# Polysketch attention into a squared-ReLU MLP: an earlier load and turn of q's second part, and two token tiles of kv sums ahead of the first q features

## The chip, the core and the metric

The kernel runs on one core of one Trainium2 chip. Five engines work beside each other, each on its own instruction stream in order: TensorE (PE, matrix products), VectorE (DVE), ScalarE (ACT), GpSimd (POOL) and SyncE (SP), which here issues nearly all DMA transfers. They wait for each other on semaphores. The metric is device time in microseconds; what is told of a kernel is the median of several runs.

## What is computed

```python
def phi(x):
    a = np.einsum('rd,bhsd->bhsr', S1, x)
    b = np.einsum('rd,bhsd->bhsr', S2, x)
    return np.einsum('bhsi,bhsj->bhsij', a, b).reshape(*x.shape[:-1], r * r)
q_p, k_p = (phi(q), phi(k))
kv = np.einsum('bhsf,bhsd->bhfd', k_p, v)
z = np.sum(k_p, axis=2)
num = np.einsum('bhsf,bhfd->bhsd', q_p, kv)
den = np.einsum('bhsf,bhf->bhs', q_p, z)[..., None] + 1e-06
attn = num / den
x = attn.transpose(0, 2, 1, 3).reshape(B * S, H * D)      # 4352 x 128
h = np.maximum(x @ w_in, 0.0)                              # w_in 128 x 2048
out = (h * h) @ w_out                                      # w_out 2048 x 128
```

There are 4 batches, 4 heads, 1088 tokens and a head size of 32; the sketches have r = 8 rows, so a token has 64 features. All inputs and the output are 32-bit floats.

## The kernel before, in words

The MLP runs over ten chunks of tokens (256, 384, 448, 448, five of 512, 256). A chunk's 2048 hidden columns are cut into units. For each unit TensorE makes x @ w_in into a PSUM tile (`pg`, line 589), ScalarE takes the ReLU (`gt`, line 598), ScalarE or VectorE squares it (`g`, lines 609 and 611), and TensorE adds its product with w_out to the chunk's sum (`po`, line 630). The attention of one batch is made beside the MLP of the tokens before it, and its result is the transposed input `xT`.

**The start, written out by hand** (lines 682 to 823). Nothing of the MLP can run before the first 256 tokens of batch 0 have gone through attention, and that needs the sums over all 1088 tokens of k and v. So the start is one chain over small pieces:

- SP issues the loads in this order: S2, k of batch 0 in two parts, the first 256 columns of q, v in eight parts (four for token tiles 0 to 3, four for tiles 4 to 8), then two quarters of w_in, a quarter of w_out, q's second part (columns 256 to 640, line 184), the rest of w_in and w_out, q's last part. Later loads follow as the planner places them. Eight semaphores are used in turn for the transfers: a transfer is issued once the one eight places before it has landed.
- `keep_warm(n)` puts n dummy products on TensorE: W0 of them first, W1 after the sketch matrices are made (line 692), W3 before the first MLP product.
- VectorE turns k (`a_kT0`, line 284, three pieces) and q's first part (`a_qT(0, 0, 8)`, line 290).
- TensorE makes the k features of the nine token tiles in four groups of 2, 2, 3 and 2 (`a_kf`, line 309); ScalarE copies one half of each (`kb`, line 315), VectorE multiplies the halves (`a_kp0`, line 325).
- `q0` (line 743) makes the sketches of the first 256 q tokens into the PSUM tile `x0`, ScalarE copies a part (`qb0`, line 754), VectorE multiplies (`qp0`, line 761).
- `a_kv0(t)` (line 389) adds one token tile's features times v to the PSUM tile `kvp`, four products for each tile.
- From `kvp`, VectorE makes `bd` (line 775) and `zm` (line 785), TensorE the denominators and numerators (`den0`, `num0`, line 798), VectorE turns, inverts and spreads the denominators (`dT0`, `rd0`, `bc0`, lines 816 to 820) and multiplies: `xT` for tokens 0 to 255 (line 821).
- POOL casts the four quarters of w_in (`cast_wi`, line 674).

The PSUM tiles of the start share two tags, `po` and `pg`, with two buffers each: a new tile of a tag waits for the readers of the tile two before it.

**The rest is planned.** A small list scheduler (`_Order`) gets tasks with an engine, an estimated duration, a key and dependencies, simulates the engines by these estimates, and emits the instructions in the order of that simulation; on the chip each engine then keeps that order. A batch's queries are handled in chunks (`AC`): batch 0 in blocks of 8, 12 and 16 (a block is 32 positions). For the chunk (0, 8): `qT` turns (line 290), sketches `qc` on TensorE (line 297), turns `qt` (475), denominators `pd`, `dn`, `rc` (481 to 495), sixteen small copies `rd` on POOL (line 503), shuffles (512) and products (527) for `qp`, numerators `nd` on TensorE (542), two turns `bc` of the inverted denominators (552), and two products into `xT` (559). These last feed the second MLP chunk, whose first `pg` product of width 384 needs both.

The task `qT` of the third chunk (0, 20) turns q's last part in two pieces (256 and 192 columns). In the order of before they stand between the two `bc` turns of chunk (0, 8).

Of the kernel before, what the change touches and what calls it, by code (L numbers as in the profile page):

```python
# [9 lines left out]
F32 = mybir.dt.float32  # L10
# [4 lines left out]
def _ap(t: bass.AP, p0: int, np_: int, off: int, free):  # L15
    p = list(t.ap)[0]
    return bass.AP(
        t.tensor, t.offset + p0 * p[0] + off, [[p[0], np_]] + [list(d) for d in free]
    )
# [85 lines left out]
def kernel(  # L105
# [11 lines left out]
    nc = tc.nc  # L117
# [7 lines left out]
    GT, G2, LA = 4, 6, 3.5  # L125
    LU = 4
    KC = [(0, 160), (160, 128)]
    W0, W1, W3 = 5, 4, 1
    ND, QT, WI, KL, QL = 2, 3.0, (1.0, 1.9), (30.0, 8.0), 4.0


# [4 lines left out]
    FC, at = [], 0  # L136
# [16 lines left out]
    psf = ctx.enter_context(tc.tile_pool(name="psf", bufs=2, space=bass.MemoryType.PSUM))  # L153
# [3 lines left out]
    def sb(name, cols, dt=F32, rows=128):  # L157
        return cpool.tile([rows, cols], dt, tag=name, name=name)
# [10 lines left out]
    s_nat, ss, s2f = sb("s_nat", 32, rows=16), sb("ss", 80), sb("s2f", 32)  # L169
# [13 lines left out]
    def load_q(eng, b, c0, c1):  # L183
        eng.dma_start(
            qn[b % 2][:, c0:c1],
            bass.AP(q.tensor, q.offset + b * H * S * D + c0, [[G * D, 128], [1, c1 - c0]]),
        )
# [16 lines left out]
    def load_wi(eng, c):  # L204
        eng.dma_start(
            w_in32[:, 512 * c : 512 * c + 512], moe_w_in[:, 512 * c : 512 * c + 512]
        )

    def load_wo(eng, c):
        eng.dma_start(  # L210
            _ap(w_o, 0, 128, 512 * c, [[128, 4], [1, 128]]),
            bass.AP(
                moe_w_out.tensor, moe_w_out.offset + c * 512 * 128,
                [[128, 128], [128 * 128, 4], [1, 128]],
            ),
        )
# [51 lines left out]
    st = {}  # L268

    def att(name):  # L270
        return psa.tile([128, 2048], F32, tag="att", name=name)

    def banks(t_, x, col, n, k=2):

        return _ap(t_, 0, 128, 512 * x + col, [[512, k], [1, n]])
# [5 lines left out]
    def a_kT0(t0, n):  # L281
        p = 3 if t0 + n > NT - 2 else 4
        i = 32 * (first(0, t0, 1) - first(0, t0, 0))
        nc.vector.transpose(
            _ap(kt0, 0, 128, 128 * t0, [[32, p], [128, n], [1, 32]]),
            _ap(kn[0], 0, 128, 32 * first(0, t0, 0), [[i, p], [32, n], [1, 32]]),
        )

    def a_qT(b, i0, n):
        nc.vector.transpose(qT[:, 32 * i0 : 32 * i0 + 32 * n], qn[b % 2][:, 32 * i0 : 32 * i0 + 32 * n])  # L290
# [31 lines left out]
    def a_kp0(t0, n):  # L322

        kf, kb = st["kf", t0]
        nc.vector.tensor_tensor(
            out=_ap(st[0, "kp"], 0, 128, 256 * t0, [[64, 4 * n], [8, 8], [1, 8]]),
            in0=_ap(kf, 0, 128, 0, [[8, 4 * n], [1, 8], [0, 8]]),
            in1=_ap(kb, 0, 128, 0, [[8, 4 * n], [0, 8], [1, 8]]),
            op=mult,
        )  # L330
# [55 lines left out]
    def a_kv0(t):  # L386
        for h in range(H):
            i, y, o, o_v = h % 2, h // 2, 64 * (H * t + h), 32 * (NT * h + t)
            nc.tensor.matmul(  # L389
                st[0, "kvp"][64 * i : 64 * i + 64, 64 * y : 64 * y + 64],  # L390
                st[0, "kp"][:, o : o + 64],
                _ap(vn[0], 0, 128, o_v, [[VC - o_v, 2], [1, 32]]),
                start=(t == 0 and y == 0),
                stop=(t == NT - 1),
                skip_group_check=True,
            )
# [171 lines left out]
    for ci, (c0, n) in enumerate(FC):  # L568
        first_unit[c0] = len(units)
        nb = 512 // n  # L570
# [120 lines left out]
    for h in range(H):  # L691
        nc.tensor.matmul(
            sp[32 * h : 32 * h + 32, 0:80], s_nat[:, :], sel[:, 80 * h : 80 * h + 80]
        )
    nc.scalar.copy(ss[:, :], sp[:, 0:80])
    load_wi(nc.sync, 0)
    load_wi(nc.sync, 1)
    load_wo(nc.sync, 0)
    load_q(nc.sync, 0, 256, 640)
    load_wi(nc.sync, 2)  # L700
    load_wi(nc.sync, 3)
    for c in range(1, 4):
# [29 lines left out]

    a_kT0(4, 3)
    a_kT0(7, 2)
    a_qT(0, 0, 8)


    x0 = att("x0")

    def q0(x):  # L740
        for y in range(2):
            r, o = slice(64 * y, 64 * y + 64), 512 * (2 * x + y)
            nc.tensor.matmul(x0[:, o : o + 256], sq[r, 128 * x : 128 * x + 128], qT[r, 0:256])  # L743

    new_kp(0)
    qb0 = wpool.tile([128, 512], F32, tag="qb0", bufs=1, name="qb0")
# [2 lines left out]
    a_kf(2, 2, psf, "pg")  # L749
    a_kf(4, 3, psf, "po")  # L750
    a_kf(7, 2, psf, "pg")
    q0(0)
    q0(1)
    nc.scalar.copy(_ap(qb0, 0, 128, 0, [[256, 2], [1, 256]]), banks(x0, 0, 0, 256))
    st[0, "kvp"] = psf.tile([128, 512], F32, tag="pg", name="kvp")
    for t0, n in ((0, 2), (2, 2), (4, 3), (7, 2)):
        a_kp0(t0, n)
        for t in range(t0, t0 + n):
            a_kv0(t)

    nc.vector.tensor_tensor(
        out=_ap(qp0, 0, 128, 0, [[256, 2], [1, 256]]), in0=banks(x0, 2, 0, 256),
        in1=_ap(qb0, 0, 128, 0, [[256, 2], [1, 256]]), op=mult,
    )
    nc.vector.transpose(s2f[:, :], _ap(ss, 0, 128, 72, [[0, 4], [1, 8]]))
    den0 = psf.tile([128, 512], F32, tag="po", name="den0")
    for y in range(2):
        nc.tensor.matmul(
# [5 lines left out]
    def a_bd(x):  # L774
        nc.vector.tensor_tensor(
            out=_ap(bd, 0, 128, 128 * x, [[64, 2], [32, 2], [1, 32]]),
            in0=_ap(st[0, "kvp"], 0, 128, 32 * x, [[64, 2], [0, 2], [1, 32]]),
            in1=_ap(own_p, 0, 128, 0, [[0, 2], [1, 2], [0, 32]]),
            op=mult,
        )  # L780
# [8 lines left out]
        op=mult,  # L789
    )  # L790
    a_bd(0)
    st["kvt"] = wpool.tile([128, 128], F32, tag="kvt", name="kvt")
    nc.scalar.copy(st["kvt"][:, :], st[0, "kvp"][:, 0:128])
    num0 = psf.tile([128, 512], F32, tag="pg", name="num0")
# [49 lines left out]
    def on(f, *args):  # L844
        return lambda eng: f(*args)

    prev = {"qc": None}
    PEL, M, T0 = 0.3, 5.0, 1.5
# [5 lines left out]
    def q_tasks(b, i0, nb, key):  # L854

        m = 16 * nb
        k0 = key - 6.0 - 8 * dve(m)
        names = []
        for x in range(2):
            i1, n1 = i0 + x * (nb // 2), nb // 2  # L860
            n1 = min(n1, G - i1)
            names.append(("qT", b, i1))
            O.add(
                names[-1], {"DVE": dve(32 * n1)}, k0 - 1.5,
                ([("qn", b)] if b else []) + prev["qTuse"], on(a_qT, b, i1, n1),
                at=QT if i0 == 20 else 0.0,
            )
        kb = KB.get((b, i0))
        O.add(
            ("qc", b, i0), {"PE": 0.75}, k0 - 1.0,  # L870
            names + [("w", b)] + ([("kT", kb, 0), ("kT", kb, 18)] if kb else []),
            on(a_qc, b, i0, nb), rings=[("att", 1)], lag=PEL,
        )
        if kb:
            glued(("kc", kb), 0.65, ("qc", b, i0), lambda eng: a_kc(kb, st[b, "qc", i0]))
        prev["qTuse"] = [("qc", b, i0)] if i0 + nb == 4 * NT else []
        for x in range(2):
            O.add(
                ("qt", b, i0, x), {"DVE": dve(m)}, k0 - 0.3 + 0.1 * x, [], on(a_qt, b, i0, nb, x),
                uses=[("qc", b, i0)], rings=[("qt", 1)] if x == 0 else [],  # L880
            )
        rc = [("rc", b, j) for j, _ in AC[b] if j < i0] or [("rc", b - 1, j) for j, _ in AC[b - 1]]
        O.add(
            ("pd", b, i0), {"DVE": dve(8 * nb)}, k0 - 0.1, rc, on(a_pd, nb),
            uses=[("qt", b, i0, 0), ("qt", b, i0, 1)],
        )
        O.add(
            ("rc", b, i0), {"DVE": 0.2 + nb * 17 / 960}, k0 - 0.1, [], on(a_rc, nb),
            uses=[("pd", b, i0)], rings=[("rc", 1)],
        )  # L890
        for c in range(4):
            O.add(
                ("rl", b, i0, c), {"POOL": 0.8}, k0 + 0.1 * c, [], on(a_rl, b, i0, nb, c),
                uses=[("rc", b, i0)], rings=[("rd", 2)] if c == 0 else [],
            )
        for w_ in ("qb", "qa0", "qa1"):
            for x in range(2):
                O.add(
                    (w_, b, i0, x), {"DVE": dve(m)}, k0, [], on(a_qs, b, i0, nb, w_, x),
                    uses=[("qc", b, i0)], rings=[(w_, 1)] if x == 0 else [],  # L900
                )
                k0 += 0.1
        for e in range(E):
            for x in range(2):
                O.add(
                    ("qp", b, i0, e, x), {"DVE": dve(m)}, k0 + 2.0, [], on(a_qp, b, i0, nb, e, x),
                    uses=[(f"qa{e}", b, i0, x), ("qb", b, i0, x)],
                    rings=[("qp", 3), ("qp", 3)] if (e, x) == (0, 0) else [],
                )
                k0 += 0.1  # L910
# [124 lines left out]
    for u in range(NU):  # L1035
# [9 lines left out]
        for i in range(m):  # L1045
# [3 lines left out]
                rings=[("pg" if u else "po", 2)] if i == 0 else [], lag=0.05,  # L1049
# [3 lines left out]
            rings=[("gt", GT)],  # L1053
# [13 lines left out]
        for j, mm in enumerate(mm2s):  # L1067
# [3 lines left out]
                rings=[("po", 2)] if d0 + j == 0 else [], lag=0.05,  # L1071
# [3 lines left out]
        if d0 + m == NB and ci != last:  # L1075
            po = [x for u_ in range(first_unit[c0], u + 1) for x in pe2[u_]]
            O.add(("oT", c0), {"DVE": dve(n)}, tu[u] + 3.0, [], on(f_oT, c0, n), uses=po,
                  rings=[("oT", 2)])
# [47 lines left out]
```

## Time and profile before

| what | value |
|---|---|
| median of 3 runs | 186.29 us (185.88 to 187.98) |
| time of the profiled execution | 185.68 us |
| its span, first to last instruction | 183.9 us |
| outside the span | 1.8 us |
| busy: PE, PE weight loads | 178.4 us (97%), 105.4 us (57%) |
| busy: ACT, DVE, POOL | 137.8 us (75%), 121.2 us (66%), 39.0 us (21%) |
| granted TensorE clock over the span | 1.000 |
| HBM read, written | 8.78 MB, 2.23 MB |

The profile is one execution, taken by the hardware profiler. Its page gives busy times and shares of the engines, the span in 40 equal slices of 4.6 us with the busy share in tenths, the chain of work that ended last, and the costliest groups of instructions. From the trace one can ask for a timeline (start, duration, engine, line, operation, tiles; instructions that follow each other are merged with a count, and the idle time before them with what ended it stands in brackets), for the waits by engine, and for single lines. Since a TensorE product overlaps the next, its start says more than its duration.

### The profile page before, as it was taken

The page shows a single profiled execution, that of the slowest core. Times are in us where ns is not written, and L with a number is a line of the kernel's source. Part 1 is how long each engine was busy: PE and PEld are TensorE (multiplying, and loading weights), DVE is VectorE, ACT ScalarE, POOL GpSimd, SP SyncE. Part 2 cuts the span into 40 slices and gives each one's busy share as a digit, 9 for nine tenths or more (in the row PEclk, how much of TensorE's full clock was granted, in tenths as well). Part 3 has the DMA queues.
Part 4 walks back from the last instruction along what each step waited for, and adds up shares of the span by engine and source line. Part 5 has one row for each costly group of instructions (what it writes and reads, how often), then busy time and mean ns, then how long its engine had stood idle before and what let it go on. Part 6 is the DMA issues. An engine that isn't in the chain of part 4 may idle for free.

```text
span 183.9 us, 3989 instructions
## 1 busy us (share of the span) xinstructions
PE 178.4 (97%) x1526; PEld 105.4 (57%) x1526; DVE 121.2 (66%) x258; ACT 137.8 (75%) x261; POOL 39.0 (21%) x157
## 2 busy tenths in 40 slices
PE   8989999989999999999999999999999999999992
PEld 2748766656555566555464554545555545555792
DVE  4969859989999972699996334997343334333640
ACT  3339969948958887699937778894777777777990
POOL 4526308418500001660008100510000000000000
PEclk9999999999999999999999999999999999999999
DMA  5799991020039700000030300003003000300121
GB/s 153 186 311 337 270 252 54 0 32 4 0 52 234 172 2 4 0 5 0 0 54 0 57 0 5 0 0 49 10 4 57 0 0 5 52 0 0 30 31 29
DMA packets 24610, 11.26 MB, mean 61 GB/s; under 512 B 17936, under 2 KB 23056, under 8 KB 24592
## 3 DMA queue, kind: packets, MB, share of 16 engines
q1 hardware_dynamic: 24416, 10.95, 25.4%
q8 instruction: 12, 0.20, 0.5%
q10 hardware_dynamic: 176, 0.07, 0.1%
q14 instruction: 6, 0.05, 0.1%
HBM read 8.78 MB, written 2.23 MB: 60 GB/s over the span
## 4 chain that ended last, share of the span: by engine, by line
PE 94%; DVE 1%; POOL 1%; ACT 0%; issue 0%
PE po L630 59%; PE pg L589 18%; PE nd L542 4%; PE po L625 2%; PE pol L625 2%; PE qc L297 2%; PE nd L407 1%; PE warm L681 1%; PE kvp L389 1%; PE qc L341 1%; PE kvp L407 1%; PE x L743 1%; POOL irep L715 1%; POOL sq L708 0%; DVE xT L559 0%
## 5 line engine op out<-in xcount | busy, mean ns | idle before, releaser
L630 PE MATMUL po<-g,w_o 128*128 128x512 f32 (+3 forms) x288 | 122.4, 546 | 0.0
L598 ACT ACTIVATE gt<-pg 128x512 f32<-128x512 f32 (+3 forms) x145 | 75.7, 568 | 31.1 <-PE pg L589 30.7
L630 PEld LDWEIGHTS po<-g,w_o 128*128 128x128 f32 x288 | 53.5, 189 | 31.0 <-issue 24.2
L589 PE MATMUL pg<-xT,w_in 128*128 128x512 f32 (+3 forms) x160 | 70.6, 521 | 0.4 <-DVE xT L821 0.4
L609 ACT ACTIVATE g<-gt 128x512 f32<-128x512 f32 (+2 forms) x104 | 61.8, 621 | 1.7
L611 DVE TENSOR_TENSOR g<-gt 128x512 f32<-128x512 f32 (+2 forms) x41 | 29.3, 716 | 38.9 <-ACT gt L598 38.1
L589 PEld LDWEIGHTS pg<-xT,w_in 128*128 128x128 f32 x160 | 29.2, 190 | 29.4 <-ACT gt L598 12.1
L503 POOL COPY rd<-rc 32x9 f32<-32x9 f32 (+2 forms) x80 | 19.2, 240 | 27.8 <-DVE rc L495 24.6
L449 POOL COPY kv<-kvt 32x64 f32<-32x64 f32 x48 | 12.5, 261 | 45.3 <-DVE kvt L426 43.1
L512 DVE STREAM_SHUFFLE qa<-qc 128x576 f32<-128x576 f32 (+2 forms) x20 | 11.8, 647 | 0.0
L527 DVE TENSOR_TENSOR qp<-qa,qb 128x576 f32<-128x576 f32 (+2 forms) x20 | 10.8, 600 | 0.0
L475 DVE STREAM_TRANSPOSE qt<-qc 128x576 f32<-128x576 f32 (+2 forms) x10 | 5.8, 609 | 6.9 <-PE qc L341 5.2
L360 DVE TENSOR_TENSOR kp<-fs 128x576 f32<-128x576 f32 x12 | 8.6, 740 | 0.0
L634 DVE STREAM_TRANSPOSE oT<-po 128x512 f32<-128x512 f32 (+3 forms) x9 | 5.9, 653 | 2.3 <-PE po L630 2.3
L542 PE MATMUL nd<-qp,kv 32*32 32x288 f32 (+2 forms) x320 | 6.8, 353 | 0.0
L559 DVE TENSOR_TENSOR xT<-nd,bc 128x576 fp32r<-128x576 f32 (+2 forms) x10 | 5.6, 602 | 1.8 <-PE nd L407 1.0
L290 DVE STREAM_TRANSPOSE qT<-qn 128x192 f32<-128x192 f32 (+3 forms) x11 | 6.0, 561 | 1.0 <-DMA qn<-in_q_dram 1.0
L512 DVE STREAM_SHUFFLE qb<-qc 128x576 f32<-128x576 f32 (+2 forms) x10 | 6.1, 649 | 0.0
L542 PEld LDWEIGHTS nd<-qp,kv 32*32 32x32 f32 x320 | 3.8, 103 | 3.7 <-issue 2.2
L552 DVE STREAM_TRANSPOSE bc<-rd 128x576 f32<-128x576 f32 (+2 forms) x10 | 5.7, 595 | 0.3 <-POOL rd L503 0.3
L625 PE MATMUL po<-w_o,g 128*128 128x128 f32 x32 | 5.8, 279 | 0.0
L625 PE MATMUL pol<-w_o,g 128*128 128x128 f32 x32 | 5.7, 275 | 0.0
(101 smaller groups left out, 89.2 us busy)
## 6 DMA issues: line engine op xcount, KB each, us to landing
kn<-in_k_dram SPq DMA_DIRECT2D x3, 544.0 KB, 7.1
qn<-in_q_dram SPq DMA_DIRECT2D x3, 544.0 KB, 9.1
vn<-in_v_dram SPq DMA_DIRECT2D x9, 144.0 KB, 7.8
w_in<-in_moe_w_in_dram SPq DMA_DIRECT2D x4, 256.0 KB, 5.3
w_o<-in_moe_w_out_dram SPq DMA_DIRECT2D x4, 256.0 KB, 5.4
out_dram<-oT SPq DMA_DIRECT2D x12, 64.0 KB, 2.0
out_dram<-oT SPq DMA_DIRECT2D x8, 56.0 KB, 2.7
out_dram<-oT SPq DMA_DIRECT2D x8, 48.0 KB, 1.9
```

What stands on the lines that cost most here:

```text
L360: nc.vector.tensor_tensor(out=_ap(st[b, "kp"], 0, 128, 64 * NT * h, [[64, NT], [8, 8], [1, 8]]), in0=_ap(fs, 0, 128, o, [[32, NT], [1, 8], ...
L449: nc.gpsimd.tensor_copy(_ap(st[b, "kv"], 32 * c, 32, 64 * h, [[32, E], [1, 32]]), _ap(st["kvt"], 32 * h, 32, 0, [[64, E], [1, 32]]),)
L503: nc.gpsimd.tensor_copy(st[b, "rd", i0][32 * h : 32 * h + 32, n * c : n * c + n], st["rc"][32 * c : 32 * c + 32, n * h : n * h + n],)
L512: nc.vector.stream_shuffle(in_=banks(st[b, "qc", i0], 2 * x, 0, m), out=_ap(st[b, which, i0], 0, 128, 2 * m * x, [[m, 2], [1, m]]), mask=m ...
L527: nc.vector.tensor_tensor(out=st[b, "qp", i0, e][:, r], in0=st[b, f"qa{e}", i0][:, r], in1=st[b, "qb", i0][:, r], op=mult,)
L542: nc.tensor.matmul(nd[32 * h : 32 * h + 32, 512 * c : 512 * c + m], kv[r, o : o + 32], qp[r, m * h : m * h + m], start=(e == 0), stop=(e = ...
L589: nc.tensor.matmul(st["pg", u][:, n * i : n * i + n], w_in[:, 128 * (d0 + i) : 128 * (d0 + i) + 128], xT[:, c0 : c0 + n],)
L598: nc.scalar.activation(gt[:, 0:w], st["pg", u][:, 0:w], Relu)
L609: nc.scalar.activation(to, of, Square)
L611: nc.vector.tensor_tensor(out=to, in0=of, in1=of, op=mult)
L625: nc.tensor.matmul(po[x // 128][:, 0:128], g[:, x : x + 128], w, start=(d == 0), stop=(d == NB - 1),)
L630: nc.tensor.matmul(po[0][:, 0:n], w, g, start=(d == 0), stop=(d == NB - 1))
```

## The change

Five things are edited. (1) The load of q's second part is issued ahead of the first two quarters of w_in and the first quarter of w_out, not behind them. (2) It is turned in one piece (384 columns) by hand, behind `a_bd(0)` in the start, and the planner's two `qT` tasks of chunk (0, 8) are left out; its `qc` task gets an earliest time of 0.4 in the planner. (3) The kv sums of the first two token tiles go ahead of `q0`, with the turn of q's first part between their feature product and the next; `kvp` takes a buffer of the tag `po`, not `pg`. (4) The turn of S2 (`s2f`) moves from behind `qp0` to the place where q's first turn was. (5) One dummy less ahead of the k features (W1), one more ahead of the first MLP product (W3).

```diff
-    W0, W1, W3 = 5, 4, 1
+    W0, W1, W3 = 5, 3, 2
...
+    load_q(nc.sync, 0, 256, 640)
     load_wi(nc.sync, 0)
     load_wi(nc.sync, 1)
     load_wo(nc.sync, 0)
-    load_q(nc.sync, 0, 256, 640)
     load_wi(nc.sync, 2)
...
     a_kT0(7, 2)
-    a_qT(0, 0, 8)
+    nc.vector.transpose(s2f[:, :], _ap(ss, 0, 128, 72, [[0, 4], [1, 8]]))
...
-    q0(0)
-    q0(1)
-    nc.scalar.copy(_ap(qb0, 0, 128, 0, [[256, 2], [1, 256]]), banks(x0, 0, 0, 256))
-    st[0, "kvp"] = psf.tile([128, 512], F32, tag="pg", name="kvp")
+    st[0, "kvp"] = psf.tile([128, 512], F32, tag="po", name="kvp")
     for t0, n in ((0, 2), (2, 2), (4, 3), (7, 2)):
         a_kp0(t0, n)
+        if t0 == 0:
+            a_qT(0, 0, 8)
         for t in range(t0, t0 + n):
             a_kv0(t)
+        if t0 == 0:
+            q0(0)
+            q0(1)
+            nc.scalar.copy(_ap(qb0, 0, 128, 0, [[256, 2], [1, 256]]), banks(x0, 0, 0, 256))
...
-    nc.vector.transpose(s2f[:, :], _ap(ss, 0, 128, 72, [[0, 4], [1, 8]]))
...
     a_bd(0)
+    a_qT(0, 8, 12)
...
-        for x in range(2):
+        for x in range(0 if (b, i0) == (0, 8) else 2):
...
-            on(a_qc, b, i0, nb), rings=[("att", 1)], lag=PEL,
+            on(a_qc, b, i0, nb), rings=[("att", 1)], lag=PEL, at=0.4,
```

What becomes of the planned part, read from the two built programs: TensorE's and POOL's orders stay the same but for the edits above. VectorE and ScalarE differ in one stretch. Before, VectorE has `bc`, `qT` (256), `qT` (192), `bc`, `xT`, `xT`; after, it has `bc`, one square `g` of 128x512, `bc`, `qT` (256), `qT` (192), `xT`, `xT`. That square, of the seventh unit of the first chunk, was ScalarE's before.

## The prediction

> **What bounds the kernel now.** I read the page first: engine rows by slice, then the chain that ended last.
>
> ```profile
> span 183.9 us, 3989 instructions
> PE   8989999989999999999999999999999999999992
> PE 94%; DVE 1%; POOL 1%; ACT 0%; issue 0%
> ```
>
> TensorE is busy in nearly every slice, and the change leaves its work alike but for one dummy moved. So only idle TensorE time can be won or added. The waits of TensorE (total, times, longest) show how little there is:
>
> ```profile
> PE warm L681 <- PEq L1110: 0.8, 1, 0.8
> PE qc L297 <- DVE kvt L426: 0.5, 1, 0.5
> PE pg L589 <- DVE xT L821: 0.4, 1, 0.4
> PE qc L297 <- ACT gt L598: 0.4, 1, 0.4
> PE x L743 <- POOL sw L721: 0.2, 1, 0.2
> ```
>
> The first lies at the start-up barrier and the second at 40 us, outside the edits: about 1.0 us is in reach. The last two releasers are misnamed: `qc` and `x` need a turn of q, as the timeline (start, duration) shows.
>
> ```profile
> 5.77 0.45 DVE L290 STREAM_TRANSPOSE qT<-qn 128x256 f32<-128x256 f32 x1 [0.30 <-DMA qn<-in_q_dram]
> 6.14 2.71 DVE L325 TENSOR_TENSOR kp<-kf,kb 128x512 f32<-128x512 f32 x4
> 6.36 1.14 PE L743 MATMUL x<-qT,sq 64*128 64x256 f32 x8 [0.24 <-POOL sw L721]
> ...
> 13.37 0.64 DVE L290 STREAM_TRANSPOSE qT<-qn 128x192 f32<-128x192 f32 x2 [0.70 <-DMA qn<-in_q_dram]
> 13.89 0.61 PE L297 MATMUL qc<-qT,sw 32*32 32x96 f32 x32 [0.37 <-ACT gt L598]
> 13.93 1.13 DVE L611 TENSOR_TENSOR g<-gt 128x256 f32<-128x256 f32 x2
> 14.02 1.52 POOL L674 CAST w_in<-w_in 128x512 fp32r<-128x512 f32 x2 [1.17 <-DMA w_in<-in_moe_w_in_dram]
> ...
> 19.20 0.37 DVE L552 STREAM_TRANSPOSE bc<-rd 128x192 f32<-128x192 f32 x1
> 19.50 0.66 DVE L290 STREAM_TRANSPOSE qT<-qn 128x256 f32<-128x256 f32 x2
> 20.48 0.38 DVE L552 STREAM_TRANSPOSE bc<-rd 128x192 f32<-128x192 f32 x1 [0.33 <-POOL rd L503]
> 20.79 0.58 DVE L559 TENSOR_TENSOR xT<-nd,bc 128x192 fp32r<-128x192 f32 x2
> 21.52 0.41 PE L589 MATMUL pg<-xT,w_in 128*128 128x384 f32 x1
> ```
>
> `x` starts 0.14 behind the first turn's end (6.22), `qc` behind the first half of the second (about 13.75); that turn waits for its load. Last, `xT` ends at 21.37 and the second chunk's first product starts 0.15 later: VectorE already gates TensorE there.
>
> **The start, to xT.** The first kv sums now stand ahead of `x` on TensorE and need all four first v loads. Its sequencer reached that wait early in the trace:
>
> ```profile
> L389 PEldq EVENT_SEMAPHORE  x2: 51/84/117, 6.4 to 6.5; - x2
> ```
>
> The wait at 6.50 took 117 ns where the other took 51, so it ended at 6.62, when the fourth load was in. These loads are issued as before. The feature product is earlier: it can start at 5.6 (behind the k turns that end at 5.47 and the turn of S2, 0.19) and takes 0.65. So v ends the wait, and TensorE starts at about 6.69, not 6.36: 0.33 lost. `x` and every later kv sum are queued behind it. Part returns: before, kv sums started at 7.44, after `x` had issued (eight passes of 0.108, to 7.23), because their buffer waited for the second feature product; that 0.2 is gone. The sum: 6.69, 16 of the 72 passes at 0.0295 (2.1 us over 71) to 7.16, `x` to 8.03, 0.05 for the switch, 55 passes to a last start at 9.70, against 9.54. The start is late by 0.16; with v in at 6.2, the feature product sets 6.36 less 0.02 and it is early by 0.18. I take +0.16, as the load order ahead of v is unchanged.
>
> What hides the rest: the k features start on the k turn (first piece done 4.63, they start 4.78), so the dummy removed there gains nothing; the added one (0.22 in a run of them) ends at about 12.65, ahead of `xT` at 12.83. The moved `s2f` has its slot before 5.6. `qp0` is done near 9.65, ahead of `kvp`. The hand-made turn (about 0.5, between 0.45 for 256 columns and 0.65 for 512) starts near 10.5, and `dT0` waits for denominators until about 11.1. Its cover is its load: in the first place of w_in, which took 4.1 us from issue at 6.36, 192 KB against 256, it lands between 9.8 and 10.5. If later than 10.6, every microsecond is paid.
>
> On SP the load passes three others, which move one slot (0.47) back and wait for other semaphores. By their old landings read against bytes (256 KB at 10.5, 512 at 12.2, 768 at 12.8, 960 at 13.35) the w_in quarters land at about 11.8 and 12.7. The cast of 0.61 ends at 12.4, needed at 12.9; the second at 13.35, needed at 14.1; w_out by 13.35, needed at 14.5. No cost, but margins of 0.5, not 2. POOL's order is unchanged.
>
> **qc.** Its 0.37 wait goes. `qc` starts at about 13.62, 0.27 earlier, with `xT` 0.16 later. That does not last: ScalarE's ReLUs are back to back from the first product on, so all are 0.16 late, and the product of the sixth unit, which needs the fourth unit's ReLU (end 15.58, then 15.74), issues at about 15.89, as before. Net zero.
>
> **VectorE behind it.** Two turns (0.64) leave ahead of the squares. The second square took 830 ns, the first 382; it started at 14.23, inside the cast from 14.02, and ended 0.27 behind that cast's end at 14.79, which is 256 columns' worth. With the start 0.16 late it could go at 14.10, again behind the cast's start, and ends as before. So everything down to `rc` and POOL's copies stands where it stood.
>
> **The new order of VectorE.** The second `bc` waits for POOL's copies, to 20.45. Before, both turns of q's last part filled that wait. Now a 512 square fills it, and the turns stand behind `bc` and ahead of `xT`: by spacing of starts, 0.33 and 0.295, together **0.62**. Queued behind are `xT` and the product of width 384, and all of TensorE behind that. ScalarE's freed 0.6 buys nothing there.
>
> **The square's price on POOL.** The trace has no 512 square beside these copies. Nearest rows: POOL's copies of the same line, alone, and beside products with two SBUF inputs:
>
> ```profile
> L503 POOL COPY rd<-rc x16: 182/186/192, 45.2 to 48.6; 32x9 f32<-32x9 f32 x16
> L503 POOL COPY rd<-rc x16: 178/296/1097, 27.4 to 33.4; 32x4 f32<-32x4 f32 x16
> ```
>
> The 1097 started beside the 1.21 us sum at L382. The square would start at 19.5 with four copies still to come. Bounds: 0, if POOL keeps its pace, and 0.53 (512 columns at the rate of the 0.27 above). I take 0.4, by the 1097. Nothing earlier than 20.45 follows from either; below zero is excluded, as the square gives POOL nothing.
>
> The Trainium skill, SBUF — State Buffer, section Who interferes with whom, says that a VectorE instruction with two SBUF inputs and a GpSimd instruction that reads SBUF exclude each other, first come first served, for a whole instruction. The 830 and 1097 ns agree; by this rule the term would be 0.53 and the sum 1.15.
>
> **Sum.** 0.62 + 0.4 = +1.0 us at the second chunk; VectorE's later work hangs on TensorE, and I find no idle cover behind. Span 183.9 to 184.9, execution 185.68 to 186.7. That execution lies 0.6 under the median, so 187.3 by the median; I say **187.2**, as a start less late takes off up to 0.1.
>
> **Rivals.**
> *The gain stays* (0.31). If v or the cast's quarter of w_in shifts by a tenth, the second square starts ahead of the cast, and is not held: VectorE's chain is then earlier by 0.65 (square of 0.38 and not 0.83, less the delay of the start). If the start is early too, by 0.18, it is 0.89, where `qc` sets it. Then the change costs -0.65 + 0.62 + (0 to 0.53), or -0.89 + the same: -0.27 to +0.5, so 186.0 to 186.8. For: the case turns at a start 0.08 late, and I have 0.16. Against: v at 6.62 is a row. Faster than before in about half of it.
>
> *The clock drops* (0.05), the slow side. The dummies' rows: five from 0.78 took 2.29 in all, each 0.43 behind the last; of those from 3.42 on, the last two start 0.22 apart. So full pace came after 3.35 us of steady work, near 4.13. Now TensorE idles from 6.1 to 6.69 and a little ahead of 4.75. If that loses full pace, the next 3.35 us do half the work: +1.7 on top of the sum, 189. It decides if idle of 0.57 us in 3.35 is too much; against it, 0.24, 0.37 and 0.48 of idle left the clock at 1.000.
> The Trainium skill, TensorE: Matmul & The Clock Gate, Part 1, has a free-running window of about 3.4 us that must be busy to open the clock and idle to close it; by that rule a gap of 0.57 closes nothing.
>
> *q late* (0.04). If the early load lands at 11.4, `dT0` and `xT` move by 0.8: on top, 188.
>
> **The numbers.** The likeliest has 0.60, with its own range 186.7 to 187.6 (0.45 to 1.3, with a tenth for the start). The range of 8 in 10 adds the kept gain and goes to 185.8; the upper end is 187.7. One per cent is 1.86 us, about what a measurement of this kernel tells from no change. All idle TensorE time in reach is 1.0, so faster by that has 0.02; slower, from the clock, a late q, or two shares of the sum together, 0.07; within it, 0.91.
>
> **What would show it.** Right: `kvp` starts near 6.7 and ahead of `x`; no wait of `qc` near 13.6; the second square still near 0.8; POOL's last `rd` near 20.9; the first 384 product near 22.5 with the longest wait of TensorE. Wrong: that product at or ahead of 21.5, a second square of 0.4, or dummies 0.43 apart later on.

## The result, and the profile after

The changed kernel takes 187.24 us in the median of 22 runs (186.43 to 187.75); 22 runs of the kernel before beside it gave 186.02 (185.42 to 189.61). The ratio is 1.0057, with a 95% interval from 1.0041 to 1.0074: slower by about 1.1 us, and within one per cent. Ratios here leave out the few slow runs that the kernel before has (189.61 is one), so they can differ a little from the quotient of two medians. The forecast was 187.2, range 185.8 to 187.7.

The profiled execution took 186.92 us with a span of 185.1, so 1.2 more than the span before. The page of the changed kernel, in the rows that were shown of the kernel before:

```profile
span 185.1 us, 3987 instructions
PE   8899899989999999999999999999999999999992
...
PE 88%; DVE 5%; POOL 2%; DMA 2%; issue 1%; SPq 0%; ACT 0%; DVEq 0%
```

TensorE is still busy nearly everywhere, but the chain that ended last now runs through VectorE and POOL for 7% of the span, where it was 2%. The waits of TensorE (total, times, longest) say where:

```profile
PE qc L297 <- DVE kvt L426: 0.8, 1, 0.8
PE warm L681 <- PEq L1113: 0.8, 1, 0.8
PE pg L589 <- DVE xT L559: 0.6, 1, 0.6
PE kvp L389 <- DVE qT L290: 0.4, 1, 0.4
PE pg L589 <- DVE xT L824: 0.2, 1, 0.2
```

The waits of `qc` near 13.9 (0.4) and of `x` (0.2) are gone. Three new or longer ones stand in their place: 0.6 ahead of the first product of width 384, 0.4 ahead of the first kv sums, and 0.8 instead of 0.5 at the `qc` of 41.8 us. (The releaser of the `kvp` row is misnamed: the sums don't read `qT`. The sequencer's wait for the fourth v load ended at 6.62, as it did before, and the sums start 0.06 behind that.) The timeline (start, duration, engine, line, operation, tiles; idle time before in brackets) shows the first two:

```profile
6.68 0.69 PE L389 MATMUL kvp<-vn,kp 128*64 128x64 f32 x16 [0.44 <-DVE qT L290]
7.29 1.13 PE L743 MATMUL x<-qT,sq 64*128 64x256 f32 x8
8.36 1.85 PE L389 MATMUL kvp<-vn,kp 128*64 128x64 f32 x56
...
14.07 0.89 DVE L611 TENSOR_TENSOR g<-gt 128x256 f32<-128x256 f32 x2 [0.95 <-ACT gt L598]
16.51 4.26 POOL L503 COPY rd<-rc 32x3 f32<-32x3 f32 x16 [0.92 <-DVE rc L495]
19.10 0.37 DVE L552 STREAM_TRANSPOSE bc<-rd 128x192 f32<-128x192 f32 x1
19.39 0.65 DVE L611 TENSOR_TENSOR g<-gt 128x512 f32<-128x512 f32 x1
20.80 0.38 DVE L552 STREAM_TRANSPOSE bc<-rd 128x192 f32<-128x192 f32 x1 [0.76 <-POOL rd L503]
21.10 0.66 DVE L290 STREAM_TRANSPOSE qT<-qn 128x256 f32<-128x256 f32 x2
21.68 0.58 DVE L559 TENSOR_TENSOR xT<-nd,bc 128x192 fp32r<-128x192 f32 x2
22.41 0.41 PE L589 MATMUL pg<-xT,w_in 128*128 128x384 f32 x1 [0.58 <-DVE xT L559]
```

Read it from the bottom. The product of width 384 starts at 22.41, 0.89 later than before. From the second `bc` to `xT` it is now 0.88, with the two turns between them, where it was 0.31: +0.57. POOL's sixteen copies take 4.26 from start to end and not 3.84: +0.42. They started 0.10 earlier than before. 0.57 + 0.42 - 0.10 is the 0.89. One copy carries the stretch of POOL, as the row of that line shows (minimum, median and longest in ns). First the two lines of the kernel before, then that of the changed one:

```profile
16.61 3.84 POOL L503 COPY rd<-rc 32x3 f32<-32x3 f32 x16 [1.07 <-DVE rc L495]
L503 POOL COPY rd<-rc x16: 177/183/367, 16.6 to 20.3; 32x3 f32<-32x3 f32 x16
...
L503 POOL COPY rd<-rc x16: 177/183/597, 16.5 to 20.6; 32x3 f32<-32x3 f32 x16
```

The copy of 367 ns is still there (368); the one of 597 comes on top. It runs from 19.49 to 20.09, beside the square from 19.39 to 20.04.

### The profile page after: what moved, and what is told of

It is laid out like the page before. It is cut to its first block, busy times and chain, and to the rows that moved or that the text cites. A ratio compares the mean times of both kernels' runs of the same rounds, so it can differ in the third digit from the quotient of the medians.

```text
span 185.1 us, 3987 instructions
## 1 busy us (share of the span) xinstructions
PE 178.9 (97%) x1526; PEld 105.2 (57%) x1526; DVE 121.6 (66%) x258; ACT 137.1 (74%) x260; POOL 39.1 (21%) x157
## 4 chain that ended last, share of the span: by engine, by line
PE 88%; DVE 5%; POOL 2%; DMA 2%; issue 1%; SPq 0%; ACT 0%; DVEq 0%
PE po L630 57%; PE pg L589 17%; PE nd L542 3%; PE po L625 2%; POOL rd L503 2%; PE pol L625 2%; DMA kn<-in_k_dram 2%; PE qc L297 1%; PE nd L407 1%; PE kvp L389 1%; DVE qT L290 1%; DVE kt L284 1%; PE qc L341 1%; DVE xT L559 1%; PE kvp L407 1%
## 5 line engine op out<-in xcount | busy, mean ns | idle before, releaser
L589 PEld LDWEIGHTS pg<-xT,w_in 128*128 128x128 f32 x160 | 29.1, 190 | 30.5 <-ACT gt L598 11.7
L512 DVE STREAM_SHUFFLE qa<-qc 128x576 f32<-128x576 f32 (+2 forms) x20 | 11.8, 650 | 0.0
L290 DVE STREAM_TRANSPOSE qT<-qn 128x576 f32<-128x576 f32 (+4 forms) x10 | 5.9, 601 | 0.0
```

What stands on the lines that cost most here:

```text
L512: nc.vector.stream_shuffle(in_=banks(st[b, "qc", i0], 2 * x, 0, m), out=_ap(st[b, which, i0], 0, 128, 2 * m * x, [[m, 2], [1, m]]), mask=m ...
L589: nc.tensor.matmul(st["pg", u][:, n * i : n * i + n], w_in[:, 128 * (d0 + i) : 128 * (d0 + i) + 128], xT[:, c0 : c0 + n],)
```

## Experiments

Eleven runs were made. Each profile is one execution; each time is a median over runs shared with the kernel before on the same chip. This table has the points that are read again and again, in us from the span's start; "full clock" is when the trace grants TensorE full speed, "first" the start of the first q-feature product or kv sum, whichever comes first, "den" the start of the first denominator product, "MLP" that of the first MLP product, "384" that of the first product of width 384. For e9 the trace holds no clock record.

| kernel | full clock | last k feature | first | den | MLP | 384 |
|---|---|---|---|---|---|---|
| before | 4.13 | 5.91 | 6.36 (x) | 9.69 | 12.82 | 21.52 |
| after | 4.62 | 6.01 | 6.68 (kv) | 10.14 | 13.27 | 22.41 |
| e1 old order | 5.69 | 6.20 | 6.52 (kv) | 9.98 | 13.11 | 21.57 |
| e2 turns in the wait | 5.59 | 6.14 | 6.79 (kv) | 10.25 | 13.38 | 22.31 |
| e3 only new order | 4.88 | 6.08 | 6.33 (x) | 9.66 | 12.79 | 22.31 |
| e4 q first | 4.37 | 5.93 | 6.15 (x) | 9.46 | 13.13 | 21.58 |
| e5 load alone | 5.90 | 6.51 | 6.66 (x) | 9.98 | 13.10 | 21.33 |
| e6 more switches | 6.15 | 6.43 | 6.58 (kv) | 10.39 | 13.51 | 21.86 |
| e7 dummies alone | 6.41 | 6.54 | 6.69 (x) | 10.00 | 13.12 | 21.55 |
| e8 load in old place | 4.56 | 5.88 | 6.51 (kv) | 9.97 | 15.08 | 25.84 |
| e9 turns behind bc | - | 6.32 | 6.46 (x) | 9.78 | 12.90 | 21.90 |
| e10 new order again | 5.29 | 6.23 | 6.38 (x) | 9.69 | 12.81 | 22.55 |
| e11 after again | 4.58 | 5.84 | 6.79 (kv) | 10.26 | 13.38 | 22.81 |

**e1_old_order**: the changed kernel, with the square of the seventh unit kept on ScalarE, by which the planner gives VectorE and ScalarE their old order.

```diff
             {"DVE": dve(w)} if u < ND else
+            {"ACT": 0.095 + w / 1200} if u == 6 else
             {"ACT": 0.095 + w / 1200, "DVE": dve(w)},
```

> The changed kernel, with the seventh unit's square held to ScalarE; that alone gives VectorE and ScalarE back their planned order of before (bc, qT, qT, bc, xT, xT), while the start stays as changed. Theory A (the order of VectorE ahead of the second chunk costs the time): the first product of width 384 at 21.6 to 21.8 us (before 21.5, changed 22.4), limited by TensorE's own lag of 0.3 from the start, and +0.2 to +0.35 us against before, a ratio of 1.001 to 1.002. Theory B (the start, late by 0.45 us at xT, costs the time, and the order only follows from it): the ratio stays at 1.005 or more.

Measured: 186.07 us (12 runs) against 186.18, ratio 1.0003 (0.9977 to 1.0028). The product of width 384 is at 21.57, POOL's copies take 3.83, the longest 375 ns, though the start is as new as in the changed kernel (den +0.29, first MLP product +0.29). So nearly the whole loss at the second chunk hangs on the new order of VectorE (0.05 is left of 0.89), and a start that is late by 0.3 hardly reaches that chunk. The wait of `qc` that is gone (13.75 here, 13.89 before) takes up about half of it; the rest stays with TensorE (the last w_in products of the first chunk start at 20.30, before at 20.17) but not with `xT`, for which the product of 384 waits.

**e2_turns_in_the_wait**: the changed kernel, where the second `bc` is put behind the two turns in the planner, so that VectorE has square, turns, `bc`, `xT`.

```diff
+    O.by_name["bc", 0, 8, 1]["deps"] += [O.by_name["qT", 0, i] for i in (20, 28)]
```

> The changed kernel, with the two turns of q's last part ahead of the second bc again, behind the square, which stays on VectorE. Theory A: POOL's last rd still ends near 20.8 us, as the square holds it up by 0.4, but the turns no longer stand behind it: the first 384 product at 21.7 to 21.9, so 0.5 to 0.7 us less than the changed kernel, a ratio of about 1.002 against before. Theory B: 1.005 or more. If the square's price on POOL were the larger part, the product would stay beyond 22.1.

Measured: 186.53 us (12 runs), ratio 1.0016 (0.9984 to 1.0048), 0.7 below the changed kernel's median. In its profile the product of 384 is still at 22.31, because this execution began later (den +0.56) and both squares near 14.2 were slow, so that POOL's copies began at 17.00, 0.49 later than in the changed kernel; without these 0.49 it would be 21.82, inside the 21.7 to 21.9 expected. POOL then took 4.25 again (longest 602 ns), with the square still beside it, and the way from the second `bc` to `xT` is short again:

```profile
17.00 4.25 POOL L503 COPY rd<-rc 32x3 f32<-32x3 f32 x16 [1.82 <-DVE rc L495]
...
19.88 0.65 DVE L611 TENSOR_TENSOR g<-gt 128x512 f32<-128x512 f32 x1
20.45 0.70 DVE L290 STREAM_TRANSPOSE qT<-qn 128x256 f32<-128x256 f32 x2
21.28 0.38 DVE L552 STREAM_TRANSPOSE bc<-rd 128x192 f32<-128x192 f32 x1
21.59 0.58 DVE L559 TENSOR_TENSOR xT<-nd,bc 128x192 fp32r<-128x192 f32 x2
```

The turns lie in VectorE's wait for POOL, and cost nothing there; the stretch of POOL stays. The interval alone would not settle it.

**e3_only_new_order**: the kernel before, with nothing but VectorE's and ScalarE's planned order of the changed kernel.

```diff
-            {"DVE": dve(w)} if u < ND else
+            {"DVE": dve(w)} if u < ND or u == 6 else
...
+    for i in (20, 28):
+        O.by_name["qT", 0, i]["deps"].append(O.by_name["bc", 0, 8, 1])
+    for x in range(2):
+        O.by_name["x", 0, 8, x]["deps"] += [O.by_name["qT", 0, i] for i in (20, 28)]
+    for i in (0, 18):
+        O.by_name["kT", 1, i]["deps"].append(O.by_name["x", 0, 8, 1])
```

> The kernel before, its start untouched, with only the planned order of the changed kernel on VectorE and ScalarE (seventh unit's square on VectorE, the turns behind the second bc). Theory A: the whole price, 0.58 for the turns and 0.4 for the square on POOL: first 384 product near 22.5 us, +0.9 to +1.1 us, a ratio of about 1.005. Theory B: within 0.2 us of before, 1.000 to 1.001.

Measured: 187.54 us (12 runs, 186.68 to 189.29), ratio 1.0096 (1.0058 to 1.0134). The product of 384 is 0.79 late at an unchanged start: 0.57 and 0.42 as in the changed kernel, less 0.20 by which POOL's copies began earlier, and all that without the early part of the change. But the span is 187.0, 2 us more than that explains, and the waits and the timeline of TensorE show an idle time that no other profile has:

```profile
PE qc L297 <- issue: 2.0, 1, 2.0
PE pg L589 <- DVE xT L559: 0.8, 1, 0.8
```

```profile
24.56 0.29 PE L297 MATMUL qc<-qT,sw 32*32 32x128 f32 x1
26.88 0.51 PE L297 MATMUL qc<-qT,sw 32*32 32x128 f32 x31 [2.03 <-issue]
```

"issue" means that the engine waited for nothing that the trace shows. In this execution the second 16 KB transfer of the DMA queue that carries instructions began at 24.46 and took 1.16; in the other twelve it began between 16.7 and 19.7. That fits a TensorE without instructions, but no run delays that transfer, so it is a suspicion. The profile isn't the only long run: five of the twelve took over 188 us. e10 is this kernel once more.

**e4_q_first**: e1's kernel, with the q features again ahead of all kv sums.

```diff
+    a_qT(0, 0, 8)
+    q0(0)
+    q0(1)
+    nc.scalar.copy(_ap(qb0, 0, 128, 0, [[256, 2], [1, 256]]), banks(x0, 0, 0, 256))
     for t0, n in ((0, 2), (2, 2), (4, 3), (7, 2)):
         a_kp0(t0, n)
-        if t0 == 0:
-            a_qT(0, 0, 8)
         for t in range(t0, t0 + n):
             a_kv0(t)
-        if t0 == 0:
-            q0(0)
-            q0(1)
-            nc.scalar.copy(_ap(qb0, 0, 128, 0, [[256, 2], [1, 256]]), banks(x0, 0, 0, 256))
```

> The changed kernel with the old planned order (as in the first of these) and with q0 ahead of all kv sums again; left of the change are the early load and turn of q's second part, the moved turn of S2 and the dummies. Theory A: the start is as before (first MLP product near 12.8 to 12.9 us), qc's wait of 0.37 is gone, qc near 13.6, and a part of it survives ScalarE's chain: -0.1 to -0.3 us against before, 0.9985 to 0.9995. If the lag of the start came from the k loads or the dummies and not from the kv sums, the first MLP product would stay near 13.2.

Measured: 185.86 us (12 runs), ratio 0.9987 (0.9962 to 1.0013). The kv sums are done 0.5 earlier than in e1, but the first MLP product is at 13.13, a miss. q's early load landed at 10.80 in this execution (9.23 in the changed kernel's), so the turn by hand kept VectorE waiting, and `dT`, queued behind it, with it:

```profile
10.83 0.58 DVE L290 STREAM_TRANSPOSE qT<-qn 128x384 f32<-128x384 f32 x1 [0.66 <-DMA qn<-in_q_dram]
11.33 0.41 DVE L817 STREAM_TRANSPOSE dT<-den 128x256 f32<-128x256 f32 x1
```

This is the rival "q late" of the prediction on a small scale (10.80, where the rival had 11.4), met by chance.

**e5_load_alone**: the kernel before, with only the load of q's second part moved ahead; every engine's order of work stays.

```diff
+    load_q(nc.sync, 0, 256, 640)
     load_wi(nc.sync, 0)
     load_wi(nc.sync, 1)
     load_wo(nc.sync, 0)
-    load_q(nc.sync, 0, 256, 640)
```

> The kernel before with one edit: q's second part is loaded ahead of w_in and w_out, as in the change; all orders of the engines stay as before, so the planner's two turns stand behind xT. Theory A: the load lands before 11 us, the turns run right behind xT at 12.7, qc's wait of 0.37 goes and with it the lag of VectorE's squares; nothing is lost at the start: qc near 13.5, the first 384 product at 21.0 to 21.4, and -0.15 to -0.4 us, a ratio of 0.998 to 0.999. Rival: ScalarE's chain or the cast of w_in's third quarter holds the same work where it was, and the ratio is 1.000.

Measured: 185.67 us (12 runs), ratio 0.9990 (0.9969 to 1.0011). The wait of `qc` is gone (13.74) and the product of 384 is at 21.33, the earliest of all. What the wait was worth, 0.2 by this one profile, is less than the runs can show.

**e6_more_switches**: e1's kernel, with the two halves of the q features parted, one behind the first kv group and one behind the second.

```diff
         if t0 == 0:
             q0(0)
+        if t0 == 2:
             q0(1)
             nc.scalar.copy(_ap(qb0, 0, 128, 0, [[256, 2], [1, 256]]), banks(x0, 0, 0, 256))
```

> The changed kernel with the old planned order, and TensorE going from kv sums to x and back twice at the start, not once (two of x's four products behind the third and fourth token tile). The work is the same. If each pair of changes between the two kinds of product costs what the changed kernel shows (0.14 into x, 0.30 out of it), the last kv sum and the first MLP product come 0.4 to 0.5 us later than in the kernel with the old order and one pair, 13.1 there. If the 0.3 were a wait for VectorE's feature products, nothing is added: within 0.1.

Measured: 186.46 us (10 runs), ratio 1.0031 (1.0017 to 1.0044), where e1 had 1.0003 (0.9977 to 1.0028). Its timeline of TensorE has the same work in more pieces:

```profile
6.58 0.69 PE L389 MATMUL kvp<-vn,kp 128*64 128x64 f32 x16
7.20 0.70 PE L743 MATMUL x<-qT,sq 64*128 64x256 f32 x4
7.83 0.69 PE L389 MATMUL kvp<-vn,kp 128*64 128x64 f32 x16
8.44 0.70 PE L743 MATMUL x<-qT,sq 64*128 64x256 f32 x4
9.07 1.39 PE L389 MATMUL kvp<-vn,kp 128*64 128x64 f32 x40
```

From the last kv pass to the first `x` it is 0.152 (kv passes follow each other in 0.0295), and from the last `x` to the next kv pass 0.306 (`x` in 0.108). One more change there and back therefore costs 0.12 + 0.20 = 0.32, and den is 0.35 later than in e1 when the later first pass (0.06) is taken off.

**e7_dummies_alone**: the kernel before, with one dummy fewer ahead of the k features and one more ahead of the first MLP product.

```diff
-    W0, W1, W3 = 5, 4, 1
+    W0, W1, W3 = 5, 3, 2
```

> The kernel before with one dummy less ahead of the k features and one more ahead of the first MLP product. Theory A: both lie in time that TensorE waits anyway: k features at 4.8 to 5.0, first MLP product near 12.8 and a ratio of 1.000 within 0.002. Rival (full pace comes later, by the missing dummy): k features or x run at half pace, the first MLP product 0.3 us late or more, and a ratio above 1.002.

Measured: 185.93 us (12 runs), ratio 0.9994 (0.9967 to 1.0022). No effect. Its k features start at 4.81, as early as before (4.78), yet last to 6.54, since the full clock came only at 6.41. With a late clock the dummy left out even helps their start: they begin at 4.81 to 4.85 with three dummies there and the clock at 5.59 or later (e1, e2, e6, e7), but at 5.23 with four and the clock at 5.29 and 5.90 (e10, e5), because the dummies too run at half pace until then.

**e8_load_in_old_place**: e1's kernel, with q's load back behind w_in and w_out, while the turn by hand stays early.

```diff
-    load_q(nc.sync, 0, 256, 640)
     load_wi(nc.sync, 0)
     load_wi(nc.sync, 1)
     load_wo(nc.sync, 0)
+    load_q(nc.sync, 0, 256, 640)
```

> The changed kernel with the old planned order, and q's second part loaded in its old place, behind the first half of w_in; the turn by hand stays ahead of dT0. If the earlier load is what keeps that turn free, it now waits for the landing near 13.4, dT0 follows at 13.9 and not at 11.3, the first MLP product at 15.6 to 15.9 and not at 13.1: +2.3 to +2.7 us against the kernel with the early load, a ratio of 1.012 to 1.015. If the turn has slack elsewhere, 1.003 or less.

Measured: 190.48 us (4 runs), ratio 1.0257 (1.0223 to 1.0292), more than expected. The turn waited for q until 12.78 (2.1 us), the first MLP product is at 15.08, earlier than expected but 2.26 later than in the kernel before, and the product of 384 at 25.84, 4.32 later. The page (40 slices of 4.7 us) and a table by windows (us, busy us of PE, PEld, DVE, ACT and POOL with counts, granted clock, DMA share, GB/s) show where the rest went:

```profile
PEclk9995799999999999999999999999999999999999
```

```profile
9.00:12.70 3.70, 3.70 (x65) 2.07 (x62) 1.20 (x4) 0.60 (x3) 1.22 (x2) 1.00 0.92 305
12.70:15.08 2.38, 0.01 (x1) 0.03 (x1) 1.98 (x5) 0.21 (x1) 1.20 (x2) 0.94 0.98 288
15.08:21.80 6.72, 6.72 (x52) 5.50 (x53) 5.37 (x25) 4.59 (x9) 2.63 (x13) 0.51 1.07 308
```

After the idle stretch the clock fell to half, from 14.80 to 21.63, and 2.1 us more were lost on the way.

**e9_turns_behind_bc**: the kernel before, with the turns behind the second `bc` as in e3, but the square of the seventh unit left on ScalarE.

```diff
             {"DVE": dve(w)} if u < ND else
+            {"ACT": 0.095 + w / 1200} if u == 6 else
...
+    for i in (20, 28):
+        O.by_name["qT", 0, i]["deps"].append(O.by_name["bc", 0, 8, 1])
...
```

> The kernel before with the two turns of q's last part behind the second bc and ahead of xT on VectorE, as in the changed kernel, but with the square of the seventh unit left on ScalarE; nothing else of the change. POOL's sixteen copies then run beside no VectorE square. Theory (the sum's two terms stand apart): xT is late by the 0.62 of the turns alone; POOL's copies take 3.84 as before, their longest 0.4 or less; the first product of width 384 starts near 22.1 (21.52 + 0.6), TensorE's longest wait on xT is about 0.3; time 0.5 to 0.7 above the kernel before, ratio 1.003. Rival 1 (the square on POOL carries the loss): the product starts within 0.2 of 21.52, ratio 1.000. Rival 2 (POOL is slow for another reason than the square): copies of over 0.5 us appear here too, product near 22.4, ratio 1.005.

Measured: 186.47 us (10 runs), ratio 1.0027 (0.9993 to 1.0062), 0.5 above the kernel before. The copies take 3.84 again and none is over 367 ns:

```profile
16.41 3.84 POOL L503 COPY rd<-rc 32x3 f32<-32x3 f32 x16 [0.80 <-DVE rc L495]
19.00 0.37 DVE L552 STREAM_TRANSPOSE bc<-rd 128x192 f32<-128x192 f32 x1
20.29 0.38 DVE L552 STREAM_TRANSPOSE bc<-rd 128x192 f32<-128x192 f32 x1 [0.91 <-POOL rd L503]
20.59 0.66 DVE L290 STREAM_TRANSPOSE qT<-qn 128x256 f32<-128x256 f32 x2
21.17 0.59 DVE L559 TENSOR_TENSOR xT<-nd,bc 128x192 fp32r<-128x192 f32 x2
```

The product of 384 is at 21.90, +0.38 and 0.2 short of what was expected, and the copies began 0.20 earlier than before: 0.58 for the turns alone. Both rivals fall, since the square on POOL isn't needed for this part, and without the square no copy is long.

**e10_new_order_again**: e3's kernel, unchanged.

> The kernel of e3_only_new_order once more, unchanged: only VectorE's and ScalarE's order of the changed kernel on the kernel before. Theory: the 2.0 us that TensorE lost at 24.6 in that profile is not part of the order, but of that execution; here the product of width 384 starts near 22.3 again, the longest wait of TensorE behind 23 us is the 0.5 at 40 us, and the span is 184.7 to 185.0. Rival: the order brings it each time; a wait of about 2 us stands between 24 and 27 again and the span is near 187.

Measured: 187.03 us (10 runs, 186.48 to 187.62), ratio 1.0040 (1.0009 to 1.0071), span 184.9. No idle time of 2 us in this execution. The longest copy is 605 ns, and the product of 384 is at 22.55, at a start like that of the kernel before.

**e11_after_again**: the changed kernel, unchanged.

> The changed kernel once more, unchanged, on the same chip as e9 and e10. Theory: ratio to before 1.005 to 1.007; POOL's longest copy 0.55 to 0.62, the product of width 384 at 22.3 to 22.5; the start (den) between 9.9 and 10.4, by when the k features get the full clock; the 0.3 between the weight load and the first qc product at 41.5 us stands again, as it follows the program. Rival: that 0.3 belongs to one execution, and the two are 0.03 apart here as in the kernel before.

Measured: 186.92 us (10 runs), ratio 1.0052 (1.0026 to 1.0078), span 185.5. The longest copy is 598 ns. The product of 384 is at 22.81, above the expected 22.5, as the fourth v load kept the first kv sums to 6.79 and den to 10.26. The 0.3 at `qc` stands again.

## Why the prediction was right, and where it wasn't

**The sum.** The forecast was +1.0 at the second chunk, 0.62 for the turns and 0.4 for POOL, and the profile has +0.89 there: 0.57, 0.42, and 0.10 back. e9 shows the first term alone (0.58, no long copy). e1, e2, e3 and e10 show both by taking them away and putting them in: with the square beside the copies the longest is 597 to 605 ns in five profiles, without it 367 to 377 in eight. The mechanism and the place were right, and the copies behind the slow one carry it to the second `bc`, as the prediction's sum had it.

**The price on POOL.** The prediction took 0.4 between the ends 0 and 0.53, guided by a copy of another shape beside a longer product; 0.42 was measured. In the changed kernel's repeat the square runs from 19.80 to 20.45, and the copy that comes at 19.89 ends at 20.49, 0.04 behind it. So the copy is held until the square is through, and the square itself isn't held: 0.65 for 512 columns. The Trainium skill, SBUF — State Buffer, section Who interferes with whom, says that a VectorE instruction with two SBUF inputs and a reading GpSimd instruction exclude each other, in order of arrival. The 597 ns agree. The price is less than the full 0.53, as the square had been running for 0.09 to 0.10 when the copy came, in all five profiles with that square.

**The start, where a term was mis-sized.** The prediction had TensorE begin at 6.69 with kv sums, when the fourth v load is in; it was 6.68, and for that reason. (In the other five profiles with this order the wait for that load ended between 6.38 and 6.74.) It then made the start late by 0.16, and it was 0.45 late (den 9.69 to 10.14). The step that failed reads: "before, kv sums started at 7.44, after `x` had issued (eight passes of 0.108, to 7.23), because their buffer waited for the second feature product; that 0.2 is gone", and, in the sum, "0.05 for the switch". That 0.2 was not a wait for a buffer. Before, the last `x` pass starts at 7.12 and the first kv pass 0.32 later:

```profile
7.44 2.32 PE L389 MATMUL kvp<-vn,kp 128*64 128x64 f32 x72
```

In e5, with the same order and the same buffer, the gap is 0.31, though the second feature product had been done for 0.24. The gap stands in the changed kernel too (last `x` pass at 8.05, next kv pass 8.36), where the buffer is another and the second feature product was done at 7.25, and e6 has it a second time for one more change. Going from kv to `x` costs another 0.12. So 0.27 more were paid than counted: 0.15 of the 0.2 thought gone, and 0.12 for the way there. The Trainium skill, TensorEngine Tiling (Array Packing), section Tiling Modes, says that a change of the tiling mode drains TensorE. The trace agrees, with 64-row `x` between 128-row sums and 0.32 for the pair; the section gives no price, and no run here tells a drain from another cost of changing.

Why it did no harm: the prediction's own step for `qc` ("Net zero") said that a start late by 0.16 is taken up by the wait that goes. That much is taken up, and no more. The second product of the sixth unit starts at 16.00 before and at 16.29 in the changed kernel, 0.29 later with a start late by 0.45; in e1, e5 and e6 it is 0.14, 0.13 and 0.54 later with a start late by 0.29, 0.28 and 0.69 (the first MLP product). (The prediction has 15.89 for this unit, "as before"; the trace before has its two products at 15.72 and 16.00.) So `qc` itself starts at 13.91 and not at 13.62. The 0.29 stays with TensorE to the end of the first chunk. It isn't paid in the changed kernel because the product of 384 waits longer still, for VectorE's `xT`: 0.58 of idle time stands ahead of it. Where `xT` is late too the rest shows: in e6 the product of 384 is 0.34 late.

**The second square.** It was to be held near 0.8 by POOL's cast again. Here the cast was earlier (13.73 to 14.35, since the quarter of w_in landed earlier) and held the first square instead, 550 ns and then 412. A held square ends 0.27 behind its cast again (14.62 behind 14.35), but this cast cost less: the two squares take 0.89 and not 1.13, from a start 0.14 later, and are done 0.10 earlier. This is the 0.10 that came back. The step was right in that a cast holds one square, wrong in which, and 0.10 off in its sum.

**The rival "the gain stays".** It counted on VectorE's chain being 0.65 earlier or more once the second square isn't held. In e9 neither square is held (426 and 419 ns), and POOL's copies begin 0.20 earlier than before. In none of the thirteen profiles is it more. What takes the rest is the next product with two inputs from SBUF, `pd`, which meets the cast of the last quarter of w_in. First the kernel before, then e9:

```profile
15.65 0.26 DVE L481 TENSOR_TENSOR pd<-qt 128x96 f32<-128x96 f32 x1
...
14.34 1.27 POOL L674 CAST w_in<-w_in 128x512 fp32r<-128x512 f32 x2 [2.64 <-DMA w_in<-in_moe_w_in_dram]
15.07 0.65 DVE L481 TENSOR_TENSOR pd<-qt 128x96 f32<-128x96 f32 x1
```

In e9 `pd` ends at 15.72, 0.11 behind that cast. It is held so in seven profiles (e1, e3, e4, e5, e6, e9 and e11, 379 to 650 ns), and ends 0.10 or 0.11 behind a cast in each. In e10 nothing of VectorE's is held there, and the copies still begin at 16.64, behind POOL's own cast (16.08 to 16.69). So the early gain of this rival was out of reach in these runs; before a freed square is counted as won, one has to look at the products behind it and at POOL's own queue.

**Loads.** The prediction put q's early load between 9.8 and 10.5. It landed at 9.23 in the changed kernel and between 8.81 and 10.80 in the seven profiles with the early load, so the forecast was too narrow on both sides; the quarters of w_in landed at 11.7 and 12.4 (forecast 11.8 and 12.7). From 10.6 on the prediction had every microsecond paid: e4 (10.80) crosses that point, and its `dT` starts 0.36 later than before, though den is 0.23 earlier.

**The clock.** The rival that TensorE loses full pace by idling 0.57 did not come: the clock over the span is 1.000. e8 shows that the mechanism is real, at 2.4 us of idle time.

**What the forecast did not have.** Between the product of 384 and the end the changed kernel loses 0.29 more, all of it at the `qc` of 41.8 us. Its weights load at 41.52 and its first product starts at 41.84, where the two are 0.03 apart before (first two lines):

```profile
40.62 0.27 PEld L297 LDWEIGHTS qc<-qT,sw 32*32 32x32 f32 x32 [0.95 <-PE pg L589]
40.65 0.78 PE L297 MATMUL qc<-qT,sw 32*32 32x288 f32 x32 [0.48 <-DVE kvt L426]
...
41.52 0.10 PEld L297 LDWEIGHTS qc<-qT,sw 32*32 32x32 f32 x1 [0.95 <-PE pg L589]
41.84 0.24 PEld L297 LDWEIGHTS qc<-qT,sw 32*32 32x32 f32 x31 [0.22 <-issue]
41.84 0.78 PE L297 MATMUL qc<-qT,sw 32*32 32x288 f32 x32 [0.78 <-DVE kvt L426]
```

This gap is 0.16 to 0.35 in the seven profiles of programs with the edited beginning (after, e1, e2, e4, e6, e8, e11) and 0.03 in the other six, so it goes with the program and not with the order of VectorE. What makes it is open. So the sum was not complete: +1.0 was forecast for the execution profiled, +0.89 came at the second chunk and 0.29 behind it, 1.18 in all, and 186.7 was forecast where 186.92 was measured. That the median of 187.24 is met more closely than that is chance. (e1 has this gap too, at its widest, 0.35, and a ratio of 1.0003 with an interval of 0.0025 to either side; a loss of that size alone is below what these runs tell apart.)

Not separated either: which share of e8's loss would remain at full clock, why five of e3's twelve runs, and none of e10's ten, took over 188 us, and why single executions of the kernel before reach 189 to 191 us.

## What to carry to other kernels

Look at what stands in an engine's wait before moving it: here two turns cost nothing while VectorE waited for POOL, and their full 0.58 once a planner had put a square in that wait and the turns behind it. Price a moved VectorE product with two SBUF inputs by what GpSimd does beside it, too: the square came to lie beside short copies that end on the critical path, and one of them grew from 0.18 to 0.60 us. And before an idle time is booked as a wait that an edit removes, find the same gap in a place where the supposed releaser was long done.

## What was not expected of the hardware

**The start of the full clock is not the kernel's.** In twelve profiles with a clock record it was granted between 4.13 and 6.41 us, with the same dummies up to 3.4 us, and once granted it lasts in steps of 3.413 us (53 of them before, 52 in e1, 3 in e8 until it fell). The k features run until 5.91 at the earliest grant and until 6.54 at the latest, and by that the first `x` of e5 and e7 stands at 6.66 and 6.69, 0.3 later than before, with TensorE's order of work unchanged but for e7's dummies. A difference of 0.3 in the start of two single profiles can be this alone. The prediction derived 3.35 us of steady work from one profile, which is a phase and not a threshold. The Trainium skill, TensorE: Matmul & The Clock Gate, Part 1, calls the window free-running and the warm-up variable from run to run; these profiles agree.

**Idle time that closes the clock.** In e8 TensorE idled from 12.70 to 15.08. The step of 3.413 that ended at 14.80 had 2.10 of idle time in it, and the clock went to half for two steps, to 21.63, although TensorE was busy from 15.08 on. The 2.03 idle in e3 fell on two steps (edges, counted from its grant at 4.88, at 21.95, 25.36 and 28.77), with 1.5 at most in one, and kept the clock. The same section of the skill has a whole idle window close it; by this one trace less is enough.
